# A two-layer MLP mixer kernel on one core: first loads ahead of the entry barrier on two rings, tile 0 started from its mean alone, two transposes fewer on TensorE, and a new order of the work

## The chip, the cores and the metric

The kernel runs on one core of one Trainium2 chip. The metric is the device time of one execution in microseconds; lower is better. The profiles record a span, from the first to the last instruction, which is 1.3 to 3.4 us shorter than the time of the same run. All runs use one core. A run is called fast or slow by its own time: slow if it is over 1.5% above the fastest run of the same kernel.

## The reference

```python
B, S, D, F = 1, 2048, 512, 1792            # bfloat16
h  = gelu(layernorm(x) @ w1)               # layer 1: D x D
c  = D // 4                                # four column groups of h are shifted along S
g0, g1, g2, g3 = shift(+1), shift(-1), shift(+2), shift(-2)
x1 = x + concat([g0, g1, g2, g3]) @ w2     # "mix"
out = x1 + gelu(layernorm(x1) @ w3) @ w4   # layer 2: "up" D x F, "down" F x D
```

S is worked on in 16 tiles of 128 rows. Layer 1 uses tile numbers 0 to 15, layer 2 the numbers 16 to 31 for the same rows (16 is row tile 0 of layer 2).

## The kernel before

The kernel lists operations, orders them on each engine with a small scheduling model, and emits them with semaphores. TensorE (PE) follows a hand-given script: `up1:N` and `up2:N` are the up-projections of the N-th group of tiles of layer 1 and layer 2 (the groups used below are single tiles at first, up to `up1:5` and `up2:1`), `mix:N` and `down:N` the products with w2 and w4 for row tile N. Each up-projection needs its normalised tile transposed, and there are two ways to do that. A tile named `ty:N` in the script is transposed on PE (four 128x128 matmuls against an identity, then a copy out of PSUM). Every other tile is transposed by a DMA that SyncE issues:

```python
if q not in pe_tp:                          # not named in the script
    pg.add("sp", f"tp{q}",
           lambda e: e.dma_start(xT[:, :, P * t : P * (t + 1)], xn_buf[:, slot(q), :], transpose=True),
           reads=[(("xn", slot(q)), q)], writes=[(("xT", t, c), layer) for c in range(DC)], queue="tp")
```

The order of the loads (all on SyncE) and the start of the script of PE:

```python
NAT = (1,)          # this tile is only centred; its scale is applied after its matmul ("by rows")
LOADS = """
x0 x2 x1 w1a w1b x3 x4-5 w2 w3 w4a tp17 w4b x6-7 x8-11 x12-15 tp8
"""
SCRIPT = """
warm:11 ty:1 ty:0 ty:2 up1:1 up1:0 th:1 up1:2 ty:3 mix:0 ty:4 mix:1 up1:3-4 mix:2 ty:16 mix:3 up2:0 up1:5
up2:1 mix:4 down:0-1 up2:2 up1:6-7 mix:6 down:3 down:2 mix:5 up1:8 ...          [cut]
"""
```

The tile in `NAT` is multiplied "by rows" (the row matmuls below), with its result not yet transposed; `th:N` transposes that result on PE. So before has six PE transposes of inputs (tiles 0 to 4 and 16); tile 5's up-projection stands behind the first of layer 2 (`up2:0`). `warm:11` are 11 matmuls on zeros. `emit` appends everything behind the entry barrier that the framework puts at the start of a program:

```python
for op in prog.seq:
    ...                                     # waits for what it needs
    ins = op.fn(engs[e])
    ins.then_inc(sems[op.stream], inc)
```

Of the kernel before, what the change touches and what calls it, by code (L numbers as in the profile page):

```python
# [6 lines left out]
P = 128  # L7
# [5 lines left out]
ENGINES = ["sp", "act", "pe", "dve", "pool"]  # L13

class Op:


    def __init__(self, name, eng, fn, reads, writes, dur, queue):
        self.name, self.eng, self.fn = name, eng, fn
        self.reads, self.writes = list(reads), list(writes)  # L20
        self.dur, self.queue = dur, queue
        self.idx = 0
        self.prio = 1e9
        self.first = None
        self.lag = 0.0

class Program:



    HOP = {"pe": 190.0, "dve": 160.0, "act": 230.0, "pool": 200.0, "sp": 70.0}
    LOOK = {"dve": 300.0, "act": 300.0}
    DUE = 6000.0

# [14 lines left out]
    def order(self):  # L49
# [13 lines left out]
        preds = [set() for _ in self.ops]  # L63
        for op in self.ops:
            d = preds[op.idx]
# [9 lines left out]
        order_only = set()  # L75
# [23 lines left out]
        while stack:  # L99
            i = stack.pop()  # L100
# [8 lines left out]
        if self.DUE:  # L109
# [15 lines left out]
            for i in reversed(topo):  # L125
# [7 lines left out]
                op.prio = late  # L133
        for op in self.ops:
            if op.first is not None:
                op.prio = op.first
# [4 lines left out]
        self.preds = preds  # L141
        npend = [len(d) for d in preds]
        ready = [0.0] * len(self.ops)
        cands = {e: [] for e in ENGINES}
        for op in self.ops:
            if npend[op.idx] == 0:
                cands[op.eng].append(op)
        free = {e: 560.0 for e in ENGINES}
        qfree = moved = 0.0
        turned = False  # L150
        out = []
        while len(out) < len(self.ops):
            best = None
            for e in ENGINES:
                if cands[e]:
                    t = max(free[e], min(ready[o.idx] for o in cands[e]))
                    if best is None or t < best[0]:
                        best = (t, e)
            t, e = best
            look = self.LOOK.get(e, 1.0)  # L160
            op = min((o for o in cands[e] if ready[o.idx] <= t + look), key=lambda o: (o.prio, o.idx))
            cands[e].remove(op)
            start = max(free[e], ready[op.idx])
            op.start = start
            if op.queue is None:
                done = free[e] = start + op.dur
            else:
                free[e] = start + (1300.0 if op.queue == "tp" else (1000.0 if e == "pool" else 460.0))
                if op.queue == "tp":
                    done = max(start + 2500.0, qfree + 1750.0)  # L170
                    qfree = max(qfree, start + 1400.0) + 600.0
                    turned = True
                else:
                    qfree = max(qfree, start + 1600.0) + op.dur
                    if turned and not op.name.startswith("out"):
                        qfree += 700.0
                        turned = False
                    moved += op.dur / 2900.0
                    done = qfree + op.lag + (350.0 if op.name.startswith("out") else min(1150.0, 250.0 + 900.0 * moved))
            out.append(op)  # L180
            for j in succs[op.idx]:
                npend[j] -= 1
                o = self.ops[j]
                hop = 70.0 if op.queue else (self.HOP[e] if o.eng != e else (0.0 if e == "pe" else 120.0))
                if (op.idx, j) not in order_only:
                    ready[j] = max(ready[j], done + hop)
                if npend[j] == 0:
                    cands[o.eng].append(o)
        self.seq = out
        for a, b in order_only:  # L190
            preds[b].discard(a)
        self.total = max(free.values())
        return out

GROUPS = {1: (1, 1, 1, 1, 1, 1, 2, 2, 2, 2, 2), 2: (1, 1, 2, 4, 4, 4)}
NORM = {5: "pool", 7: "act", 10: "pool", 11: "act", 18: "act", 19: "pool", 20: "pool"}
EVAC = {1: "both", 4: "both", 16: "dve"}
SQRT = ()
STAT_ACT = (1, 5, 6, 16, 18, 21)
HALF = ()  # L200
TAIL = (256, 128, 128)
VPE = {3: "pool", 4: "pool", 5: "pool", 6: "pool", 18: "pool", 19: "pool", 21: "pool"}
NMR = {1: "pool", 4: "pool", 5: "pool", 18: "pool", 20: "pool", 21: "pool"}
NAT = (1,)
HEV = {1: "dve", 4: "dve"}
LOADS = """
x0 x2 x1 w1a w1b x3 x4-5 w2 w3 w4a tp17 w4b x6-7 x8-11 x12-15 tp8
"""
SCRIPT = """
warm:11 ty:1 ty:0 ty:2 up1:1 up1:0 th:1 up1:2 ty:3 mix:0 ty:4 mix:1 up1:3-4 mix:2 ty:16 mix:3 up2:0 up1:5  # L210
up2:1 mix:4 down:0-1 up2:2 up1:6-7 mix:6 down:3 down:2 mix:5 up1:8 mix:8 mix:7 up1:9 mix:9-10 up1:10 mix:12
mix:11 up2:3 mix:14-15 up2:4 mix:13 down:5-6 down:9 down:7-8 down:4 up2:5 down:10 down:12 down:14 down:11
down:13 down:15
"""

def bass_standalone__mixer_s_mlp__prompt_kernel(nc, x, w1, w2, w3, w4, out):
# [14 lines left out]
    with ExitStack() as es:  # L231
# [62 lines left out]
        def load(item):  # L294
            name, _, eng = item.partition("@")
            eng = eng or "sp"
            if name[0] == "x":
# [8 lines left out]
                else:  # L306
                    yield pg.add(eng, f"dma_x{t0}",
                                 lambda e: e.dma_start(x_sb[:, t0:t1, :], xt[:, t0:t1, :]),
                                 writes=[(("x", t, hh), 0) for t in range(t0, t1) for hh in (0, 1)],
                                 dur=(t1 - t0) * 380.0, queue=eng)  # L310
            else:
# [6 lines left out]
                             writes=[((name[:2], c), 0) for c in range(c0, c1)],  # L318
                             dur=(c1 - c0) * P * src.shape[1] * 2 / 345.0, queue=eng)
                op.lag = 900.0 if name[:2] == "w2" else 0.0  # L320
                yield op
# [300 lines left out]
        pe_tp = {n for kind, n in steps if kind in ("tp", "ty")}  # L622
        queue = []
        for item in LOADS.split():
            if item[:2] == "tp":
                if int(item[2:]) not in pe_tp:
                    queue.append(item)
            else:
                for op in load(item):
                    op.first = len(queue) - 100  # L630
                    if op.eng == "sp":
                        queue.append(op.name)
        for t in range(NT):
            ln(1, t)
        for kind, n in steps:
# [10 lines left out]
            else:  # L646
                for _ in mm_up(int(kind[2]), n):
                    pass
        pg.line(queue)
        pg.order()  # L650
        emit(nc, es, pg)

def emit(nc, es, prog):
# [4 lines left out]
    for op in prog.seq:  # L658
        if op.queue is not None:
            op.stream = ("dma", ndma)  # L660
            sems[op.stream] = es.enter_context(nc.semaphore(f"sem_dma{ndma}"))
            ndma += 1
        else:
            op.stream = op.eng
    know = {e: {} for e in ENGINES}
    implied = {}
    count = {}
    last_write, readers = {}, {}
    for op in prog.seq:
# [19 lines left out]
        for s, v in sorted(needs.items(), key=lambda sv: -sv[1]):  # L689
# [6 lines left out]
            k[s] = max(k.get(s, 0), v)  # L696
        ins = op.fn(engs[e])
        inc = 1 if op.queue is None else 16
        ins.then_inc(sems[op.stream], inc)
# [6 lines left out]
        for res, ver in op.writes:  # L706
            last_write[res] = (op.stream, val, ver)
            readers[res] = []
    for op in prog.seq:
        if op.name.startswith("out_dma"):  # L710
            nc.sync.wait_ge(sems[op.stream], 16)
# [28 lines left out]
```

## Time and profile before

| | before |
|---|---|
| time, median of 4 runs | 137.95 us (136.35 to 138.11) |
| span of the profile | 135.2 us |
| PE busy | 97% |
| PE uninterrupted in the chain of waits | from 16.2 to 133.3 us |

The timeline of before for PE (start in us, duration in us, line, operation, count, and the idle time before with what ended it):

```profile
1.17 4.15 PE L604 MATMUL o_ps<-zeros 128*128 128x512 bf16 x11 [1.17 <-DVE zeros L281]
5.23 1.25 PE L437 MATMUL y_ps<-ident,xn_buf 128*128 128x128 bf16 x12
6.49 1.02 PE L455 MATMUL y_ps<-w_sb,xnT 128*128 128x512 bf16 x4
...
10.36 1.02 PE L551 MATMUL o_ps<-w_sb,hT 128*128 128x512 bf16 x4 [0.49 <-DVE vpe L349]
...
12.31 1.95 PE L511 MATMUL y_ps<-xnT,w_sb 128*128 128x128 bf16 x32
...
16.04 7.31 PE L511 MATMUL y_ps<-xnT,w_sb 128*128 128x128 bf16 x128
```

The warm-up ends near 5.3 us, the first real matmul starts at 6.49, the first mix at 10.36, and layer 2 at about 16. From there PE never stops. The chain of waits of before says the same (start, duration, what):

```profile
15.34 0.86 PE o_ps L551 x4
16.21 7.15 PE y_ps L511 x128
...
115.11 18.21 PE o_ps L580 x112
```

So only the head and the tail can be shortened. The first bn_stats on VectorE, and the issue table (size of one, median us from issue to landing):

```profile
2.83 1.29 DVE L363 BATCH_NORM_STATS2 st<-x_sb 128x6 f32<-128x512 bf16 x2 [1.71 <-DMA x_sb<-in_x_dram]
```

```profile
w_sb<-in_w_dram SPq DMA_DIRECT2D x1, 1792.0 KB, 10.3
...
xnT<-xn_buf SPq DMA_TRANSPOSE x26, 2.5
```

### The profile page before, as it was taken

What the parts mean: (1) busy time and instruction counts of PE and PEld (TensorE: products, weight loads), DVE (VectorE), ACT (ScalarE), POOL (GpSimd) and SP (SyncE); (2) the same over time, 40 slices, a digit from 0 to 9 for tenths busy, and PEclk for the clock granted to TensorE, in tenths of its full rate; (3) what the DMA queues carried; (4) which work ended last, traced back from release to release, by engine and by line L of the source; (5) the groups of instructions that cost most, each with busy time, mean ns of one, the idle gap of its engine ahead of it and who ended that gap; (6) DMA issues with size and microseconds to landing.
All of it is one profiled execution on the core that took longest, in us unless ns stands there. A gap on an engine that the chain in (4) does not pass through costs nothing.

```text
span 135.2 us, 2125 instructions
## 1 busy us (share of the span) xinstructions
PE 131.5 (97%) x855; PEld 73.5 (54%) x855; DVE 58.0 (43%) x164; ACT 49.4 (37%) x68; POOL 22.9 (17%) x52
## 2 busy tenths in 40 slices
PE   6999999999999999999999999999999999999994
PEld 2476799448874466644444444444444444444463
DVE  2986750799936359995008200622202200032222
ACT  4786377613941053325552555100000666300000
POOL 2355242233561011151000200100000000000000
DMA  4899979955654510404500120031110200011112
GB/s 120 283 314 379 298 114 330 298 87 116 122 112 83 116 41 0 82 0 84 110 0 0 39 43 0 0 78 39 39 39 13 67 2 0 0 39 39 39 39 78
DMA packets 22344, 12.44 MB, mean 92 GB/s; under 512 B 14912, under 2 KB 21824, under 8 KB 22336
## 3 DMA queue, kind: packets, MB, share of 16 engines
q1 hardware_dynamic: 21904, 12.19, 36.4%
q10 hardware_dynamic: 432, 0.13, 0.4%
q8 instruction: 6, 0.10, 0.3%
q14 instruction: 2, 0.02, 0.0%
HBM read 6.82 MB, written 2.10 MB: 66 GB/s over the span
## 4 chain that ended last, share of the span: by engine, by line
PE 95%; DVE 2%; POOL 1%; issue 1%; DVEq 0%
PE y_ps L511 44%; PE o_ps L580 36%; PE o_ps L551 10%; PE o_ps L604 3%; POOL rstd L381 1%; PE y_ps L437 1%; DVE st L363 0%; POOL vpe L370 0%; DVE xn_buf L393 0%; DVE mv L345 0%; DVE vpe L349 0%; DVE o_sb L588 0%; DVE zeros L281 0%; DVE xnT L443 0%; DVE mv L365 0%
## 5 line engine op out<-in xcount | busy, mean ns | idle before, releaser
L511 PE MATMUL y_ps<-xnT,w_sb 128*128 128x128 bf16 (+2 forms) x496 | 63.6, 288 | 0.0
L511 PEld LDWEIGHTS y_ps<-xnT,w_sb 128*128 128x128 bf16 x496 | 40.7, 98 | 23.0 <-issue 0.4
L580 PE MATMUL o_ps<-w_sb,h2T 128*128 128x512 bf16 (+2 forms) x252 | 49.1, 355 | 0.0
L526 ACT ACTIVATE h2T<-y_ps 128x1024 bf16<-128x1024 f32 (+2 forms) x29 | 28.8, 995 | 44.0 <-PE y_ps L511 44.0
L580 PEld LDWEIGHTS o_ps<-w_sb,h2T 128*128 128x128 bf16 x252 | 23.6, 98 | 25.2
L588 DVE TENSOR_TENSOR o_sb<-o_ps,x_sb 128x512 bf16<-128x512 f32 (+2 forms) x18 | 11.4, 632 | 39.6 <-PE o_ps L580 37.6
L381 POOL TENSOR_TENSOR rstd<-vpe,neghalf 128x1 f32<-128x1 f32 x32 | 17.5, 558 | 59.7 <-DVE vpe L370 41.9
L562 DVE TENSOR_TENSOR x_sb<-o_ps,x_sb 128x512 bf16<-128x512 f32 x13 | 8.9, 690 | 24.9 <-PE o_ps L551 24.9
L363 DVE BATCH_NORM_STATS2 st<-x_sb 128x6 f32<-128x512 bf16 x26 | 17.5, 686 | 1.9 <-DMA x_sb<-in_x_dram 1.7
L551 PE MATMUL o_ps<-w_sb,hT 128*128 128x512 bf16 x64 | 15.8, 379 | 0.5 <-DVE vpe L349 0.5
L393 DVE TENSOR_SCALAR xn_buf<-x_sb,mv,rstd 128x512 bf16<-128x512 bf16 x24 | 9.6, 410 | 3.4 <-POOL rstd L381 2.7
L526 ACT ACTIVATE hT<-y_ps 128x512 bf16<-128x512 f32 (+1 forms) x10 | 8.1, 809 | 7.9 <-PE y_ps L511 7.8
L551 PEld LDWEIGHTS o_ps<-w_sb,hT 128*128 128x128 bf16 x64 | 6.0, 98 | 6.1 <-DVE vpe L349 0.6
L338 ACT ACTIVATE junk<-x_sb 128x512 bf16<-128x512 bf16 x6 | 3.7, 624 | 9.5 <-DVE x_sb L558 9.4
L604 PE MATMUL o_ps<-zeros 128*128 128x512 bf16 x11 | 4.2, 552 | 1.2 <-DVE zeros L281 1.2
L365 DVE BATCH_NORM_AGGREGATE mv<-st 128x2 f32<-128x6 f32 x26 | 4.1, 173 | 0.3
L370 DVE TENSOR_SCALAR vpe<-mv 128x1 f32<-128x1 f32 x23 | 3.1, 149 | 0.3
L604 PEld LDWEIGHTS o_ps<-zeros 128*128 128x128 bf16 x11 | 1.4, 132 | 3.5 <-issue 2.2
L405 POOL TENSOR_SCALAR xn_buf<-x_sb,rstd,nmr 128x512 bf16<-128x512 bf16 x4 | 3.1, 768 | 0.3
L442 ACT ACTIVATE xnT<-y_ps 128x512 bf16<-128x512 bf16 (+1 forms) x5 | 2.4, 513 | 1.1 <-PE y_ps L437 1.1
L402 ACT ACTIVATE xn_buf<-x_sb,nmr,rstd 128x512 bf16<-128x512 bf16 x3 | 2.4, 806 | 1.1 <-DVE nmr L398 1.1
L558 DVE SCALAR_TENSOR_TENSOR x_sb<-o_ps,x_sb 128x512 bf16<-128x512 f32 x3 | 2.1, 690 | 1.3 <-PE o_ps L551 1.3
(33 smaller groups left out, 20.6 us busy)
## 6 DMA issues: line engine op xcount, KB each, us to landing
out_dram<-o_sb SPq DMA_DIRECT2D x15, 128.0 KB, 1.7
w_sb<-in_w_dram SPq DMA_DIRECT2D x1, 1792.0 KB, 10.3
w_sb<-in_w_dram SPq DMA_DIRECT2D x2, 896.0 KB, 9.5
x_sb<-in_x_dram SPq DMA_DIRECT2D x2, 512.0 KB, 8.1
x_sb<-in_x_dram SPq DMA_DIRECT2D x4, 128.0 KB, 2.1
w_sb<-in_w_dram SPq DMA_DIRECT2D x2, 256.0 KB, 3.1
x_sb<-in_x_dram SPq DMA_DIRECT2D x2, 256.0 KB, 4.7
w_sb<-in_w_dram SPq DMA_DIRECT2D x1, 512.0 KB, 6.2
```

Source lines behind the costliest of these rows:

```text
L338: (lambda d: (lambda e: e.activation(d, src, ACT_F.Square, accum_out=sums[:, q, 1:2])))(junk[:, b, :]),
L363: pg.add("dve", f"bnst{q}", lambda e: e.bn_stats(st6[:, q, :], src), reads=rs, writes=[(("st6", q), 0)], dur=605)
L365: pg.add("dve", f"bnag{q}", lambda e: e.bn_aggr(mv[:, q, :], st6[:, q, :]), reads=[(("st6", q), 0)], writes=[(("mv", q), 0)], dur=75)
L381: lambda e: e.tensor_tensor(col(rstd), col(vpe), neghalf[:], ALU.pow),
L393: lambda e: e.tensor_scalar(dst, src, mv[:, q, 0:1], rstd[:, q : q + 1], ALU.subtract, ALU.mult),
L511: ins = e.matmul(y_ps[:, p, W * i : W * (i + 1)], wsb[:, dc, P * fc : P * (fc + 1)], src[:, dc, P * t0 : P * t0 + W], start=(dc == 0), sto ...
L526: (lambda d, s: (lambda e: e.activation(d, s, ACT_F.Gelu_apprx_tanh)))(dst, ysrc),
L551: ins = e.matmul(dst, hT[:, j, c0 : c0 + P], w2_sb[:, j, :], start=(j == 0), stop=(j == DC - 1))
L562: f = lambda e: e.tensor_tensor(x1_sb[:, t, :], dst, x_sb[:, t, :], ALU.add)
L580: ins = e.matmul(dst, h2T[:, fc, P * t : P * (t + 1)], w4_sb[:, fc, cs], start=(fc == 0), stop=(fc == FC - 1))
L588: (lambda d, c: (lambda e: e.tensor_tensor(o_sb[:, oi, c], d, x1_sb[:, t, c], ALU.add)))(dst, cs),
L604: ins = e.matmul(o_ps[:, b, :], zeros[:, 0:P], zeros[:], start=True, stop=True)
```

## The change

Its intent: start the loads before the entry barrier and from two issuers (each issuing engine has a queue of its own, called its ring below; `@act` in the list of loads means ScalarE's), begin PE's real work with a tile that needs only its mean, save PE two transposes, and let a search find the rest of the order with a finer model of the DMA rings.

```diff
+    BEGIN = {"sp": 30.0, "act": 150.0, "pe": 400.0, "dve": 150.0, "pool": 450.0}
+    ENTRY = (1900.0, 2150.0)
 ...                                          [the scheduling model is rewritten; cut]
-GROUPS = {1: (1, 1, 1, 1, 1, 1, 2, 2, 2, 2, 2), 2: (1, 1, 2, 4, 4, 4)}
+GROUPS = {1: (1, 1, 1, 1, 1, 1, 2, 4, 1, 1, 2), 2: (1, 1, 2, 4, 4, 4)}
 ...                                          [NORM, EVAC, VPE, NMR, BIAS tables; cut]
-STAT_ACT = (1, 5, 6, 16, 18, 21)
-NAT = (1,)
+STAT_ACT = (0, 2, 6, 8, 10, 11, 12, 13, 23, 24, 25, 26, 28)
+NAT = (0,)
 LOADS = """
-x0 x2 x1 w1a w1b x3 x4-5 w2 w3 w4a tp17 w4b x6-7 x8-11 x12-15 tp8
+x1@act x0 x2@act w1b w1a x4 w2b@act w2a x3 x5 w3@act tp1 tp1 tp15 tp0 x8-10@act x14-15@act x13 x11-12@act
+tp1 x6-7@act w4@act
 """
 SCRIPT = """
-warm:11 ty:1 ty:0 ty:2 up1:1 up1:0 th:1 up1:2 ty:3 mix:0 ty:4 mix:1 up1:3-4 mix:2 ty:16 mix:3 up2:0 up1:5
+warm:3 warm:1 ty:0 up1:0 ty:1-2 th:0 up1:1-2 mix:0 ty:3 mix:1 up1:3-4 mix:2 up1:5 mix:3-4 up2:0-2 up1:6
 ...
+    listed = nc.m.functions[0].blocks[0].instructions
+    entry = next(i for i, ins in enumerate(listed) if type(ins).__name__ == "InstDrain")
 ...
+        if op.start < prog.ENTRY[0]:
+            ahead = len(listed)
 ...
+    listed[entry:ahead] = listed[body:ahead] + listed[entry:body]
```

The two PE transposes that go are those of tiles 4 and 16.

More of the change, by code (lines that the diff above doesn't have):

```diff
@@ L24, in __init__ @@
         self.first = None
-        self.lag = 0.0
 class Program:
-    HOP = {"pe": 190.0, "dve": 160.0, "act": 230.0, "pool": 200.0, "sp": 70.0}
+    HOP = {"pe": 200.0, "dve": 155.0, "act": 220.0, "pool": 120.0, "sp": 70.0}
     LOOK = {"dve": 300.0, "act": 300.0}
-    DUE = 6000.0
+    DUE = 3377.81
+    BEGIN = {"sp": 30.0, "act": 150.0, "pe": 400.0, "dve": 150.0, "pool": 450.0}
+    ENTRY = (1900.0, 2150.0)
     def __init__(self):
@@ L134, in order @@
         for op in self.ops:
+            op.prio += BIAS.get(op.name, 0.0)
             if op.first is not None:
@@ L141, in order, with place @@
         self.preds = preds
-        npend = [len(d) for d in preds]
+        out = self.place(succs, order_only)
+        for a, b in order_only:
+            preds[b].discard(a)
+        return out
+    def place(self, succs, order_only):
+        npend = [len(d) for d in self.preds]
         ready = [0.0] * len(self.ops)
@@ L147, in order, with finish @@
                 cands[op.eng].append(op)
-        free = {e: 560.0 for e in ENGINES}
-        qfree = moved = 0.0
-        turned = False
+        free = dict(self.BEGIN)
+        rings = {"sp": [], "act": []}
+        clock = moved = self.total = 0.0
         out = []
-        while len(out) < len(self.ops):
-            best = None
-            for e in ENGINES:
-                if cands[e]:
-                    t = max(free[e], min(ready[o.idx] for o in cands[e]))
-                    if best is None or t < best[0]:
-                        best = (t, e)
+        def finish(limit):
+            nonlocal clock
+            while True:
+                heads = {e: r[0] for e, r in rings.items() if r}
+                if not heads:
+                    return None
+                live = [e for e in heads if heads[e][0] <= clock]
+                later = min([h[0] for h in heads.values() if h[0] > clock], default=1e18)
+                if not live:
+                    if later > limit:
+                        return None
+                    clock = later
+                    continue
+                first = min(live, key=lambda e: heads[e][1])
+                step = heads[first][1] * len(live)
+                ends = clock + step <= min(later, limit)
+                if not ends:
+                    step = min(later, limit) - clock
+                for e in live:
+                    heads[e][1] -= step / len(live)
+                clock += step
+                if ends:
+                    return rings[first].pop(0)[2]
+                if clock >= limit:
+                    return None
@@ new lines, in release, with land @@
+        def release(op, o, at):
+            npend[o.idx] -= 1
+            if at is not None:
+                ready[o.idx] = max(ready[o.idx], at)
+            if npend[o.idx] == 0:
+                cands[o.eng].append(o)
+        def land(op):
+            nonlocal moved
+            if op.queue == "tp":
+                at = max(clock + 500.0, op.start + 2450.0)
+            elif op.name.startswith("out"):
+                at = clock + 300.0
+                self.total = max(self.total, at)
+            else:
+                moved += op.dur
+                at = clock + 650.0 + min(450.0, 0.25 * moved) + (1200.0 if op.dur > 1400.0 else 0.0)
+            for j in succs[op.idx]:
+                if (op.idx, j) not in order_only:
+                    release(op, self.ops[j], at + 30.0)
@@ L159, in order @@
+        while len(out) < len(self.ops):
+            while True:
+                best = None
+                for e in ENGINES:
+                    if cands[e]:
+                        t = max(free[e], min(ready[o.idx] for o in cands[e]))
+                        if best is None or t < best[0]:
+                            best = (t, e)
+                op = finish(best[0] if best else 1e17)
+                if op is None:
+                    break
+                land(op)
             t, e = best
@@ L163, in order @@
             start = max(free[e], ready[op.idx])
+            if start >= self.ENTRY[0]:
+                start = max(start, self.ENTRY[1])
             op.start = start
-            if op.queue is None:
-                done = free[e] = start + op.dur
-            else:
-                free[e] = start + (1300.0 if op.queue == "tp" else (1000.0 if e == "pool" else 460.0))
-                if op.queue == "tp":
-                    done = max(start + 2500.0, qfree + 1750.0)
-                    qfree = max(qfree, start + 1400.0) + 600.0
-                    turned = True
-                else:
-                    qfree = max(qfree, start + 1600.0) + op.dur
-                    if turned and not op.name.startswith("out"):
-                        qfree += 700.0
-                        turned = False
-                    moved += op.dur / 2900.0
-                    done = qfree + op.lag + (350.0 if op.name.startswith("out") else min(1150.0, 250.0 + 900.0 * moved))
@@ L180, in order @@
-            out.append(op)
-            for j in succs[op.idx]:
-                npend[j] -= 1
-                o = self.ops[j]
-                hop = 70.0 if op.queue else (self.HOP[e] if o.eng != e else (0.0 if e == "pe" else 120.0))
-                if (op.idx, j) not in order_only:
-                    ready[j] = max(ready[j], done + hop)
-                if npend[j] == 0:
-                    cands[o.eng].append(o)
+            out.append(op)
+            if op.queue:
+                tp = op.queue == "tp"
+                free[e] = start + (1300.0 if tp else 460.0)
+                rings[e].append([start + (1400.0 if tp else 1000.0), 600.0 if tp else op.dur, op])
+                for j in succs[op.idx]:
+                    if (op.idx, j) in order_only:
+                        release(op, self.ops[j], None)
+            else:
+                free[e] = start + op.dur
+                for j in succs[op.idx]:
+                    o = self.ops[j]
+                    hop = self.HOP[e] if o.eng != e else (0.0 if e == "pe" else 120.0)
+                    release(op, o, None if (op.idx, j) in order_only else start + op.dur + hop)
@@ L189, in order @@
+        while (op := finish(1e17)) is not None:
+            land(op)
         self.seq = out
-        for a, b in order_only:
-            preds[b].discard(a)
-        self.total = max(free.values())
-        return out
-GROUPS = {1: (1, 1, 1, 1, 1, 1, 2, 2, 2, 2, 2), 2: (1, 1, 2, 4, 4, 4)}
-NORM = {5: "pool", 7: "act", 10: "pool", 11: "act", 18: "act", 19: "pool", 20: "pool"}
-EVAC = {1: "both", 4: "both", 16: "dve"}
+        return out
+GROUPS = {1: (1, 1, 1, 1, 1, 1, 2, 4, 1, 1, 2), 2: (1, 1, 2, 4, 4, 4)}
@@ L198 @@
+NORM = {6: "pool", 7: "act", 8: "pool", 10: "pool", 12: "act", 13: "pool", 14: "pool", 20: "pool", 21: "pool", 23: "pool", 24: "pool", 25: "pool", 27: "act", 28: "act", 29: "act", 31: "pool"}
+EVAC = {0: "dve", 1: "both", 4: "dve", 5: "dve", 6: "dve", 8: "dve", 9: "both", 10: "dve", 12: "both", 13: "both", 15: "both", 19: "dve", 20: "dve", 22: "dve", 23: "dve", 24: "dve", 26: "dve", 27: "both", 28: "dve", 29: "dve", 30: "dve", 31: "dve"}
 SQRT = ()
-STAT_ACT = (1, 5, 6, 16, 18, 21)
+STAT_ACT = (0, 2, 6, 8, 10, 11, 12, 13, 23, 24, 25, 26, 28)
@@ L200 @@
 HALF = ()
 TAIL = (256, 128, 128)
-VPE = {3: "pool", 4: "pool", 5: "pool", 6: "pool", 18: "pool", 19: "pool", 21: "pool"}
-NMR = {1: "pool", 4: "pool", 5: "pool", 18: "pool", 20: "pool", 21: "pool"}
-NAT = (1,)
-HEV = {1: "dve", 4: "dve"}
+VPE = {1: "pool", 2: "pool", 3: "pool", 4: "pool", 6: "pool", 7: "pool", 9: "pool", 10: "pool", 12: "pool", 13: "pool", 14: "pool", 17: "pool", 18: "pool", 19: "pool", 21: "pool", 22: "pool", 25: "pool", 26: "pool", 27: "pool", 28: "pool", 30: "pool"}
+NMR = {1: "pool", 2: "pool", 5: "pool", 8: "pool", 10: "pool", 11: "pool", 13: "pool", 15: "pool", 18: "pool", 21: "pool", 22: "pool", 25: "pool", 26: "pool", 29: "pool", 31: "pool"}
@@ L206 @@
+NAT = (0,)
+HEV = {1: "dve", 2: "dve", 3: "dve"}
+BIAS = {"bnst19": 1806.98, "bnst3": 919, "bnst5": -1528.57, "bnst6": -755, "mean16": -61, "msq15": -99, "nmr2": -416.496, "rstd11": -131, "rstd18": 1533, "rstd22": 450, "ssq4": 250, "vpe0": -916.1, "vpe11": 651, "vpe19": 1017.92, "vpe7": 264, "x1_0": 1177}
 LOADS = """
-x0 x2 x1 w1a w1b x3 x4-5 w2 w3 w4a tp17 w4b x6-7 x8-11 x12-15 tp8
+x1@act x0 x2@act w1b w1a x4 w2b@act w2a x3 x5 w3@act tp1 tp1 tp15 tp0 x8-10@act x14-15@act x13 x11-12@act
+tp1 x6-7@act w4@act
@@ L208 @@
 """
 SCRIPT = """
-warm:11 ty:1 ty:0 ty:2 up1:1 up1:0 th:1 up1:2 ty:3 mix:0 ty:4 mix:1 up1:3-4 mix:2 ty:16 mix:3 up2:0 up1:5
-up2:1 mix:4 down:0-1 up2:2 up1:6-7 mix:6 down:3 down:2 mix:5 up1:8 mix:8 mix:7 up1:9 mix:9-10 up1:10 mix:12
-mix:11 up2:3 mix:14-15 up2:4 mix:13 down:5-6 down:9 down:7-8 down:4 up2:5 down:10 down:12 down:14 down:11
-down:13 down:15
+warm:3 warm:1 ty:0 up1:0 ty:1-2 th:0 up1:1-2 mix:0 ty:3 mix:1 up1:3-4 mix:2 up1:5 mix:3-4 up2:0-2 up1:6
+down:1 mix:5 up1:7 mix:6 down:3 mix:9 up1:8 mix:7-8 up1:9 mix:11 mix:10 up1:10 mix:12 down:0 up2:3 mix:15
@@ L214 @@
+mix:14 up2:4 mix:13 down:5 down:4 down:2 down:9 up2:5 down:8 down:7 down:13 down:6 down:11 down:10 down:12
+down:14-15
 """
@@ L309, in load @@
                                  writes=[(("x", t, hh), 0) for t in range(t0, t1) for hh in (0, 1)],
-                                 dur=(t1 - t0) * 380.0, queue=eng)
+                                 dur=(t1 - t0) * 430.0, queue=eng)
             else:
@@ L318, in load @@
                              writes=[((name[:2], c), 0) for c in range(c0, c1)],
-                             dur=(c1 - c0) * P * src.shape[1] * 2 / 345.0, queue=eng)
-                op.lag = 900.0 if name[:2] == "w2" else 0.0
+                             dur=(c1 - c0) * P * src.shape[1] * 2 / (300.0 if src.shape[1] == D else 380.0), queue=eng)
                 yield op
@@ L622, in bass_standalone__mixer_s_mlp__prompt_kernel @@
         pe_tp = {n for kind, n in steps if kind in ("tp", "ty")}
-        queue = []
-        for item in LOADS.split():
+        queues = {"sp": [], "act": []}
+        for i, item in enumerate(LOADS.split()):
             if item[:2] == "tp":
                 if int(item[2:]) not in pe_tp:
-                    queue.append(item)
+                    queues["sp"].append(item)
             else:
                 for op in load(item):
-                    op.first = len(queue) - 100
-                    if op.eng == "sp":
-                        queue.append(op.name)
+                    op.first = i - 100
+                    queues[op.eng].append(op.name)
         for t in range(NT):
@@ L648, in bass_standalone__mixer_s_mlp__prompt_kernel @@
                     pass
-        pg.line(queue)
+        for queue in queues.values():
+            pg.line(queue)
         pg.order()
@@ L664, in emit @@
             op.stream = op.eng
+    listed = nc.m.functions[0].blocks[0].instructions
+    entry = next(i for i, ins in enumerate(listed) if type(ins).__name__ == "InstDrain")
+    body = len(listed)
+    ahead = body
     know = {e: {} for e in ENGINES}
```

## The prediction

> **What bounds the kernel.** TensorE (PE). The page gives PE 97% of a 135.2 us span; the chain of waits puts 95% of the span on PE. In that chain PE is never held up after 16.2 us: 117.1 us of matmuls run to 133.3 us, at 0.86 us for four 512-column matmuls and 12.1 us for 56 up-projection matmuls of 512 columns. From these durations I count about 124.9 us of useful matmuls, 7.9 us of them before 16.2 us. So what can be won lies in the first 16.2 us (8.3 us there are warm-up, transposes and waits) and in the 1.9 us tail, which the change leaves alone.
>
> **The head, by the timeline.** Nothing is issued before about 0.72 us (the entry barrier). SyncE issues the first three x loads from 0.73 us at 0.45 us each; the first bn_stats starts at 2.83 us, the ScalarE sum of tile 1 at 3.88 us. The 11 warm-up matmuls fill 1.17 to 5.3 us, spaced 0.43 us until about 4.5 us. The first real matmul starts at 6.49 us. The chain up to 10.36 us runs through normalisation on VectorE and GpSimd, not loads.
>
> **What the change does.**
> 1. First loads issued before the barrier: about 0.7 us earlier; with two issuers x0, x1, x2 leave by about 0.6 us instead of 2.1. The Trainium skill ("DMA: Bandwidth & Descriptors", Issuing engines are not separate DMA queues) says a second issuer saves only issue time, as all share the same 16 DMA engines; at the roughly 300 GB/s of the early slices I expect w1 landed near 5 us, against 5 to 5.6.
> 2. Tile 0 comes first, needing only its mean (ScalarE 0.63 + 0.19 us, VectorE 0.15 and 0.35): first transpose near 4.1 to 4.6 us, first real matmul near 5.2 us, instead of 6.49. -1.3 us.
> 3. Two PE transposes fewer (one left to the DMA): 2 x 0.22 = -0.4 us, part of it hidden in waits.
> 4. Costs: tile 3 and w2 land later (ScalarE issues loads between early activations), tiles 4 and 5 depend on DMA transposes (2.5 us each in the issue table).
> 5. Warm-up falls from 11 to 4 matmuls: about 1.7 us, then about 2 us idle. The skill ("TensorE: Matmul & The Clock Gate", part 1) says the clock is half-rate until a sustained window of about 3.4 us; this trace agrees: spacing 0.43 us for 3.3 us, then shorter. So the first real work may run at half rate, up to about 1.5 us lost, partly inside other waits.
>
> Sum: about -2 us ideal; +0.5 us for late landings and the cold clock on average. Nothing changes after 20 us.
>
> **Predicted time: 136.0 us** (before 137.82), range 134.0 to 137.8. Faster by over 2%: 0.25; within 2%: 0.67; slower: 0.08.
>
> **What would show it.** First DMA issue near 0 us in the timeline; first real matmul at 5.0 to 5.5 us; chain of waits: PE without interruption from about 16 to 17 us with one more up-projection tile and one more mix done by then; four PE transposes. A cold clock would show as 1.7 us for tile 0's four row matmuls instead of 0.86.
>
> **What would make it wrong.** ScalarE delayed by DMA issues or its 1.28 us table load, so tile 0's sum starts after 4 us; PE cold until about 10 us; waits for DMA transposes before the second-layer groups at 16 to 30 us; or the head filling completely (over 3 us gained).

## More of the kernel before

The view of one source line gives the spread that the issue table hides. For the 26 DMA transposes of before:

```profile
L411 SPq DMA_TRANSPOSE xnT<-xn_buf x26: 1189/1264/2149, 12.2 to 87.9; - x26
DMA to landing us min/median/max: 2.4/2.5/7.6
```

The first of them (issued at 12.2 us, while w3 and w4 are still being loaded) took 6.8 us and landed at 18.9. That is late, but in this order nobody is waiting for it: it is tile 5's, whose up-projection stands behind `up2:0`. Of the 26, four were issued before 27 us and took 3.2 to 7.6 us; the other 22 took 2.4 to 4.0.

Table by stage of before (us, the stretch's length, then busy us of each engine with instruction counts, granted PE clock, share of DMA time, GB/s):

```profile
10.00:15.00 5.00, 4.64 (x49) 3.25 (x50) 3.37 (x13) 3.29 (x8) 2.39 (x5) 1.00 1.01 378
15.00:20.00 5.00, 5.00 (x80) 4.53 (x79) 3.19 (x11) 2.38 (x4) 1.63 (x5) 1.00 1.06 156
20.00:25.00 5.00, 5.00 (x70) 4.05 (x67) 0.89 (x3) 3.92 (x7) 0.95 (x2) 1.00 1.05 328
```

## The result and the profile after

The time went up, to 144.11 us (median of 4 runs, 143.44 to 144.49), against 137.95 of before. The ratio is 1.048, with a 95% interval of 1.041 to 1.055. A ratio is the mean time of one kernel's fast runs over that of the other's of the same rounds, so it is not quite the ratio of the medians. The result lies outside the predicted range.

The timeline of after for PE:

```profile
0.53 1.89 PE L658 MATMUL o_ps<-zeros 128*128 128x512 bf16 x4 [0.53 <-DVE zeros L336]
4.16 0.61 PE L491 MATMUL y_ps<-ident,xn_buf 128*128 128x128 bf16 x4 [1.74 <-DVE xn_buf L443]
5.38 1.86 PE L509 MATMUL y_ps<-w_sb,xnT 128*128 128x512 bf16 x4 [0.61 <-DVE mv L396]
...
10.97 0.81 PE L605 MATMUL o_ps<-w_sb,hT 128*128 128x512 bf16 x3
...
12.70 1.06 PE L565 MATMUL y_ps<-xnT,w_sb 128*128 128x128 bf16 x16
17.41 1.89 PE L565 MATMUL y_ps<-xnT,w_sb 128*128 128x128 bf16 x16 [3.65 <-DMA xnT<-xn_buf]
...
28.78 11.16 PE L565 MATMUL y_ps<-xnT,w_sb 128*128 128x128 bf16 x128 [0.51 <-DMA xnT<-xn_buf]
```

The first real matmul is at 5.38 us, as predicted. But tile 0's four row matmuls take 1.86 us, against 1.02 for those of tile 1 in before, and the first mix starts near 10.8, no earlier than in before (the line shows three of its four matmuls; the first is missing from the trace). Then, after tile 3, PE stands idle for 3.65 us for a DMA transpose, and the next matmuls also take twice as long (1.89 against 1.06 for the same 16). PE is uninterrupted only from 28.8 us. The chain of waits of after shows what it hangs on:

```profile
9.66 7.70 DMA xnT<-xn_buf
17.36 0.05 issue
17.41 1.89 PE y_ps L565 x16
19.29 1.72 PE o_ps L605 x4
...
23.25 5.48 DMA xnT<-xn_buf
28.73 0.05 issue
28.78 11.16 PE y_ps L565 x128
```

Tile 4's transpose is issued at 9.66 and lands at 17.36. The issue table still gives 2.5 us as the median; the view of the source line, for the three transposes issued between 9 and 15.5 us (tiles 4, 5 and 16), gives 7.7 to 10.1:

```profile
xnT<-xn_buf SPq DMA_TRANSPOSE x28, 2.5
```

```profile
L465 SPq DMA_TRANSPOSE xnT<-xn_buf x3: 1233/1258/1274, 9.7 to 14.7; - x3
...
  PE y_ps L565: 4.0, 2
...
DMA to landing us min/median/max: 7.7/8.7/10.1
```

By stage, after (columns as above; the clock is the third number from the end). The clock of the cold start does not show in this column: it is 1.00 in the stages before 10 us too, where the row matmuls took 1.86 us.

```profile
10.00:15.00 5.00, 3.65 (x43) 2.52 (x41) 3.84 (x9) 2.39 (x4) 1.43 (x3) 1.00 1.05 288
15.00:20.00 5.00, 2.59 (x19) 2.04 (x20) 0.32 (x1) 0.60 (x1) 0.00 (x0) 0.62 1.14 263
20.00:25.00 5.00, 4.45 (x27) 2.77 (x27) 3.15 (x7) 2.26 (x7) 1.58 (x4) 0.70 1.20 206
```

From 15 to 20 us VectorE, ScalarE and GpSimd are almost idle as well. The kernel gives each of them its instructions in a fixed order, and the next ones belong to tiles behind the stall. That is how one late transpose makes the next ones late: tile 17's transpose leaves only at 23.25, after the delayed mix 2 in VectorE's order. PE's clock falls to 0.62 after the idle stretch. The Trainium skill ("TensorE: Matmul & The Clock Gate", part 1) describes this: half rate after an idle window of about 3.4 us, full rate after a busy one. The trace agrees with the two states, not with the length: the matmuls ran at half rate until about 22.9 us, 5.5 us after the work resumed, and the granted clock was 0.50 already from 16.2 us, 2.4 us into the idle stretch.

The start holds another surprise. The first instruction on ScalarE that reads x in after:

```profile
2.80 0.63 ACT L387 ACTIVATE junk<-x_sb 128x512 bf16<-128x512 bf16 x1 [0.29 <-PEq L786]
```

It was released by the barrier (the releaser "PEq" is PE's sequencer), although the trace shows x0 landed at 2.17 us. In before the barrier opens at 0.72 us and x0 lands at 2.81. The loads now go ahead of the barrier, but so do four warm-up matmuls (until 2.42 us) and ScalarE's 1.28 us table load (its first activation ends at 2.51), and the barrier opens only when they are done. The statistics therefore start at 2.80 instead of 2.83.

### The profile page after: what moved, and what is told of

Its sections match the earlier page's. It is cut to its first block, busy times and chain, and to the rows that moved or that the text cites. A ratio compares the mean times of both kernels' runs of the same rounds, so it can differ in the third digit from the quotient of the medians.

```text
span 143.0 us, 2121 instructions
## 1 busy us (share of the span) xinstructions
PE 132.9 (93%) x828; PEld 73.8 (52%) x840; DVE 53.2 (37%) x150; ACT 57.6 (40%) x94; POOL 31.5 (22%) x73
## 4 chain that ended last, share of the span: by engine, by line
PE 83%; DMA 9%; DVE 3%; issue 1%; POOL 1%; ACT 1%
PE y_ps L565 39%; PE o_ps L634 34%; DMA xnT<-xn_buf 9%; PE o_ps L605 8%; PE y_ps L509 1%; DVE st L417 1%; PE y_ps L491 1%; ACT junk L387 1%; DVE xnT L497 1%; DVE x_sb L616 0%; POOL rstd L435 0%; POOL vpe L424 0%; DVE xn_buf L447 0%; DVE xn_buf L443 0%; DVE o_sb L642 0%
## 5 line engine op out<-in xcount | busy, mean ns | idle before, releaser
L565 PE MATMUL y_ps<-xnT,w_sb 128*128 128x128 bf16 (+2 forms) x493 | 65.9, 295 | 4.6 <-DMA xnT<-xn_buf 4.5
L605 PE MATMUL o_ps<-w_sb,hT 128*128 128x512 bf16 x60 | 16.2, 397 | 0.4 <-DVE mv L419 0.2
L580 ACT ACTIVATE hT<-y_ps 128x512 bf16<-128x512 f32 (+1 forms) x11 | 8.3, 752 | 18.5 <-PE y_ps L565 18.5
L417 DVE BATCH_NORM_STATS2 st<-x_sb 128x6 f32<-128x512 bf16 x19 | 12.9, 686 | 2.5 <-PEq L786 2.3
L447 DVE TENSOR_SCALAR xn_buf<-x_sb,mv,rstd 128x512 bf16<-128x512 bf16 x15 | 7.9, 524 | 5.2 <-POOL rstd L435 4.9
L459 POOL TENSOR_SCALAR xn_buf<-x_sb,rstd,nmr 128x512 bf16<-128x512 bf16 x11 | 8.5, 775 | 1.8 <-DVE nmr L452 1.7
L392 ACT ACTIVATE junk<-x_sb 128x512 bf16<-128x512 bf16 x13 | 8.1, 621 | 1.6 <-DVE x_sb L612 1.6
L424 POOL TENSOR_SCALAR vpe<-mv 128x1 f32<-128x1 f32 x13 | 3.1, 236 | 17.9 <-DVE mv L419 14.5
L456 ACT ACTIVATE xn_buf<-x_sb,nmr,rstd 128x512 bf16<-128x512 bf16 x5 | 4.0, 809 | 5.3 <-POOL nmr L452 2.8
L387 ACT ACTIVATE junk<-x_sb 128x512 bf16<-128x512 bf16 x8 | 5.0, 623 | 0.3 <-PEq L786 0.3
L612 DVE SCALAR_TENSOR_TENSOR x_sb<-o_ps,x_sb 128x512 bf16<-128x512 f32 x5 | 3.5, 692 | 1.4 <-PE o_ps L605 1.4
L491 PE MATMUL y_ps<-ident,xn_buf 128*128 128x128 bf16 x16 | 2.0, 287 | 1.7 <-DVE xn_buf L443 1.7
L491 PEld LDWEIGHTS y_ps<-ident,xn_buf 128*128 128x128 bf16 x16 | 1.6, 130 | 3.4 <-DVE xn_buf L443 2.6
```

Of the source, the lines that this page charges most:

```text
L387: (lambda d: (lambda e: e.activation(d, src, ACT_F.Copy, accum_out=sums[:, q, 0:1])))(junk[:, b, :]),
L392: (lambda d: (lambda e: e.activation(d, src, ACT_F.Square, accum_out=sums[:, q, 1:2])))(junk[:, b, :]),
L417: pg.add("dve", f"bnst{q}", lambda e: e.bn_stats(st6[:, q, :], src), reads=rs, writes=[(("st6", q), 0)], dur=605)
L447: lambda e: e.tensor_scalar(dst, src, mv[:, q, 0:1], rstd[:, q : q + 1], ALU.subtract, ALU.mult),
L459: f = lambda e: e.tensor_scalar(dst, src, rstd[:, q : q + 1], nmr[:, q : q + 1], ALU.mult, ALU.add)
L565: ins = e.matmul(y_ps[:, p, W * i : W * (i + 1)], wsb[:, dc, P * fc : P * (fc + 1)], src[:, dc, P * t0 : P * t0 + W], start=(dc == 0), sto ...
```

## The experiments

Theories. **T1**: a DMA transpose issued while bulk loads are in flight lands 6 to 10 us later, not 2.5; the change made PE depend on such transposes. **T2**: the second ring is to blame (transposes on the SyncE ring beside loads on the ScalarE ring). **T3**: the transposes are late for another reason. Besides these, the half clock could be a cause of its own: after the stall, or at the start, where only 4 warm-up matmuls are left. The diffs below show the changed part of a line only.

### e1: tiles 4 and 5 back on PE

```diff
-ty:3 mix:1 up1:3-4 mix:2 up1:5
+ty:3 mix:1 ty:4 up1:3-4 ty:5 mix:2 up1:5
```

> The kernel after, with tiles 4 and 5 of the first layer transposed on PE instead of by DMA. Theory T1 (DMA transposes issued while bulk loads are in flight land 7 to 10 us later instead of 2.5, and PE starves for tiles 4 and 5): the 3.65 us idle before the up-projection of tile 4 and the half clock after it go away, second layer starts near 19 to 20 us instead of 25, time 137 to 140 us. Rival T2 (PE starves because of something else in the new order, tile 4 only shows it): another wait takes its place in the same 13 to 20 us, time still above 142.

Measured: 143.91 us, ratio 1.046 (1.036 to 1.056). The wait for tile 4 is gone, and another has taken its place. The timeline of e1 for PE:

```profile
23.80 15.90 PE L565 MATMUL y_ps<-xnT,w_sb 128*128 128x128 bf16 x184 [4.40 <-DMA xnT<-xn_buf]
```

This is layer 2's first tile (16), whose transpose was issued at 15.58 and landed at 23.67, 8.1 us later. By the words put down beforehand it is the rival that came true (called T2 there, but not the T2 above): another wait took the place, and the time stayed above 142. The time prediction of T1 failed; its mechanism is still there, one transpose further on. Tile 16 is the other PE transpose that the change removed.

### e2: dummy matmuls in the stall

Seventeen matmuls on zeros are put between the up-projections of tiles 3 and 4, outside the schedule, so that the order of all other engines is unchanged.

```diff
+        if op.name == "up1_3_0":
+            s, v, _ = last_write[("x1", 0)]
+            engs["pe"].wait_ge(sems[s], v)
+            for _ in range(17):
+                prog.fill(engs["pe"])       # one 128x512 matmul on zeros
```

> The kernel after, with 17 dummy matmuls on zeros put into the idle time of PE before tile 4's up-projection; order of all other engines unchanged. If the half clock after the stall costs time of its own (T1): the matmuls at 17 to 23 us run at full rate, the row of them takes about 2.6 us less, tile 17's normalisation comes earlier, and the time falls by 1 to 2.5 us to about 142 us. If the half clock is only a symptom and the transposes set the pace: within 0.5 us of 144.1.

Measured: 144.74 us, ratio 1.051 (1.039 to 1.062). PE's mean granted clock was 1.000 in all four runs (0.976 to 0.988 in those of after), and no time was gained. The profile is of a slow run, and tile 4's transpose landed even later in it (20.14 us). The three fast runs (143.48, 144.68, 144.80; mean 144.32 against 144.04 of after) show no gain either. So the half clock after the stall is a symptom: the transposes set the pace.

### e3: w3 behind the transposes

w3 and all later loads go on the SyncE ring: w3 behind tiles 4 and 5, the rest behind tiles 16 and 17.

```diff
-w2a x3 x5 w3@act tp1 tp1 tp15 tp0 x8-10@act x14-15@act x13 x11-12@act
-tp1 x6-7@act w4@act
+w2a x3 x5 tp4 tp5 w3 tp16 tp17 x6-7 w4 x8-10 x11-12 x13 x14-15
```

> The kernel after, with w3 and all later loads on the SyncE ring behind the DMA transposes of tiles 4 and 5 (w3) and of tiles 16 and 17 (the rest). T1: with no bulk load in flight the transposes of tiles 4 and 5 land within 2.5 to 4 us of their issue, PE is not idle over 1 us before tile 4; w3 then lands later, near 18 to 19 us, and the time is 137 to 140 us. If the transposes are slow for another reason than bulk loads (T3): they still take over 6 us to land and the idle stays.

Measured: 148.25 us, ratio 1.080 (1.070 to 1.089), so the time was mispredicted by 8 us. The transposes behaved as T1 says. The view of the source line in e3 for the two issued between 9 and 12.1 us:

```profile
L464 SPq DMA_TRANSPOSE xnT<-xn_buf x2: 1220/1245/1270, 9.5 to 10.9; - x2
...
DMA to landing us min/median/max: 2.4/2.5/2.5
```

The same two tiles, issued at about the same time as in after (9.54 and 10.90 us, against 9.66 and 11.36), land in 2.5 us when nothing else is in flight; T3 falls. The time was lost elsewhere: w3 came at 20.97, and tiles 18 and 19, issued from 25.65 behind w4, again took 7.8 and 6.2 us, which ends in a wait of 6 us in the timeline of e3 for PE:

```profile
34.05 10.12 PE L564 MATMUL y_ps<-xnT,w_sb 128*128 128x256 bf16 x72 [6.02 <-ACT junk L391]
```

The releaser named there is a ScalarE instruction long done; the transposes landed at 33.42 and 33.92. So the new order of the loads had only moved them into the way of later transposes.

### e4: the same fault put into before

```diff
-ty:3 mix:0 ty:4 mix:1
+ty:3 mix:0 mix:1
```

> The kernel before, with only tile 4's PE transpose left to the DMA, all on the one SyncE ring. T1 (any bulk load in flight, whatever ring): tile 4's transpose lands 6 to 8 us after its issue, near 18 us, PE idles 3 to 5 us before tile 4 and then runs at half clock for some us; time 142 to 146 us. Rival T2 (only the interleaving of two rings makes the transposes slow): it lands in 2.5 to 3.5 us and the time stays within 1 us of 137.9.

Measured: 145.60 us median, with one fast run at 142.88 (before in the same rounds: 137.97 median) and three slow ones at 145.47 to 146.08. The fast run alone is 3.6% above before's median; it is one run, so it has no interval. Its mean granted clock was 0.988 (0.998 to 1.000 in the fast runs of before), which fits a stall with half clock after it there too. The profile (of a slow run) shows the wait on the single ring, in the source view for two transposes and in the timeline for PE:

```profile
  PE y_ps L511: 5.6, 1
...
DMA to landing us min/median/max: 6.0/6.9/7.9
```

```profile
18.71 1.89 PE L511 MATMUL y_ps<-xnT,w_sb 128*128 128x128 bf16 x16 [5.64 <-DMA xnT<-xn_buf]
```

One `ty:4` less in before reproduces the stall and the doubled matmul time without a second ring, so T2 is not needed. The packet records of the trace show one difference, though: on the one ring the transpose's first packet comes at 14.70 us, when the ring has nearly worked off the loads ahead of it; on two rings, in after, transpose and loads run side by side (see the last section).

### e5: only the barrier part, in before

The three first x loads, constants and 3 of the 11 warm-up matmuls go ahead of the barrier.

```diff
-warm:11 ty:1
+warm:3 warm:8 ty:1
+        if op.start < 1900.0:
+            ahead = len(listed)
+    listed[entry:ahead] = listed[body:ahead] + listed[entry:body]
```

> The kernel before with one thing of the change alone: the three first x loads, the constants and 3 of the 11 warm-up matmuls put ahead of the entry barrier; order on every engine unchanged. If the earlier start of the loads carries through to the chain of the head: first bn_stats about 0.7 us earlier in the span than 2.83, time 0.4 to 0.9 us less than before. If the head is bound by later loads or by the engines: same within 0.3 us.

Measured: 137.14 us, ratio 0.998 (0.993 to 1.003): the same. bn_stats starts at 2.31 instead of 2.83 (at the barrier's release), but the halves of w1, issued after a barrier that now opens near 2.3, land at 5.06 and 5.76, as in before (5.03 and 5.83). In the profile layer 2 starts at 15.62 instead of 16.04, a gain too small for these runs to show.

### e6: all transposes of the loading time on PE

```diff
-ty:3 mix:1 up1:3-4 mix:2 up1:5 mix:3-4 up2:0-2
+ty:3 mix:1 ty:4 up1:3-4 ty:5 mix:2 ty:16 up1:5 mix:3-4 ty:17 up2:0-2
```

> The kernel after with the transposes of tiles 4 and 5 of layer 1 and of tiles 0 and 1 of layer 2 (16, 17) all on PE, so that no DMA transpose is needed until about 25 us. T1: the 4 us wait of e1_ty45 for tile 16 goes too, no DMA-transpose wait over 1 us is left before 26 us, second layer starts near 19.5 us, time 139 to 140.5 us; what is left above before is the half clock of the first 9 to 10 us. If another wait takes its place: above 142 us.

Measured: 139.55 us, ratio 1.015 (1.008 to 1.022). The first DMA transpose is issued at 20.25. The timeline of e6 for PE:

```profile
19.07 6.42 PE L565 MATMUL y_ps<-xnT,w_sb 128*128 128x128 bf16 x112
25.92 8.02 PE L565 MATMUL y_ps<-xnT,w_sb 128*128 128x256 bf16 x72 [0.43 <-ACT junk L387]
```

Layer 2 starts at 19.07 instead of 24.98 and only 0.43 us of waiting is left there. The mean of the fast runs falls from 144.04 (after) to 139.52: 4.5 of the roughly 6.4 us (144.04 less 137.65, the mean of before's fast runs beside e6; after was run in other rounds).

### e7: e6 with a longer warm-up

```diff
+        if op.name == "tp0":
+            for _ in range(5):
+                prog.fill(engs["pe"])
```

> e6_ty4_5_16_17 with 5 more warm-up matmuls between the barrier and the first transpose; order of every other engine unchanged. If the short warm-up costs time (half clock until 9 to 10 us): the four row matmuls of tile 0 take about 0.9 us instead of 1.86, second layer starts 1.5 to 2.5 us earlier than in e6, time 137 to 138.5 us. If the half clock is hidden in waits for data: within 0.5 us of e6.

Measured: 138.41 us, ratio 1.006 (1.000 to 1.013); 1.07 us less than e6 by the means of the fast runs (138.45 and 139.52). The timeline of e7 for PE:

```profile
6.15 1.18 PE L509 MATMUL y_ps<-w_sb,xnT 128*128 128x512 bf16 x4 [0.61 <-DVE mv L396]
```

The row matmuls take 1.18 instead of 1.89 us, but start 0.2 us later than in e6, where they waited for w1, and 0.8 us later than in after: the cold filler is itself in the way. Layer 2 starts at 18.56 us, 0.5 us earlier than in e6 and not the expected 1.5 to 2.5. With no more DMA stalls the short warm-up seems to cost about 1 us, but the fast runs of e6 (138.96 to 140.01) and e7 (137.74 to 139.22) overlap, so this is not settled.

### e8: exactly the two removed transposes back

```diff
-ty:3 mix:1 up1:3-4 mix:2 up1:5
+ty:3 mix:1 ty:4 up1:3-4 mix:2 ty:16 up1:5
```

> The kernel after with exactly the two PE transposes back that the change takes away (tiles 4 and 16). If those two alone are the cause: second layer starts near 19.5 us, time 139 to 140.5. If the new order (tile 5's up-projection ahead of the second layer, its transpose by DMA under load) shares in it: PE waits 2 to 5 us for tile 5's transpose, landing at 17 to 20 us, time 140.5 to 143.

Measured: 140.11 us in one fast run, 144.41 to 145.92 in three slow ones (median 144.88). The profile is of a slow run: the timeline for PE shows tile 5 stuck, its transpose issued at 11.85 and landed at 22.01.

```profile
22.06 1.89 PE L565 MATMUL y_ps<-xnT,w_sb 128*128 128x128 bf16 x16 [5.95 <-DMA xnT<-xn_buf]
```

This is inconclusive as to shares. The fast run agrees with the first expectation (139 to 140.5), while the slow profile shows the stall of the second. The mean granted clock tells the same: 1.000 in the fast run, 0.976 to 0.988 in the three others, so here "slow" most likely means that the transpose came late, as it did in three of four runs. What it does show is that in this order tile 5 can become the next victim.

### e9, e11 and e12: attempts at a version better than both

e9 takes the change's start (barrier, two rings for the first loads, tile 0 first), 3 extra warm-up matmuls behind the barrier and, from the first mixes on, the order of before, with most of its tables and its order of the later loads; e11 puts w3 and the first half of w4 on the ScalarE ring; e12 is e11 with 5 instead of 3 extra warm-up matmuls.

```diff
 e9:  x1@act x0 x2@act w1b w1a x4 w2b@act w2a x3 x5 w3 w4a tp17 w4b x6-7 x8-11 x12-15
 e11: x1@act x0 x2@act w1b w1a x4 w2b@act w2a x3 x5 w3@act w4a@act tp17 w4b x6-7 x8-11 x12-15
+SCRIPT: warm:3 warm:1 ty:0 up1:0 ty:1-2 th:0 up1:1-2 mix:0 ty:3 mix:1 ty:4 up1:3-4 mix:2 ty:16 mix:3 up2:0 up1:5 ...
```

> A version meant to beat both: the change's start (first loads ahead of the barrier on two rings, tile 0 first by its mean, 3 more warm-up matmuls after the barrier) with everything after the first two mixes as in before: PE transposes of tiles 4 and 16, tile 5 behind the second layer's first tile, loads of w3 and w4 on the SyncE ring as in before. Head: first real matmul near 5.4 us, second layer's first tile 0.3 to 1.0 us earlier than before's 16.2, no wait for a DMA transpose over 0.5 us; time 0.3 to 1.0 us less than before. If the earlier start is taken back by later landings of w2 and of tiles 3 to 5: same as before within 0.3 us.

> e9_hybrid with w3 and the first half of w4 on the ScalarE ring instead of the SyncE ring, nothing else moved on VectorE, GpSimd and PE. If sharing the DMA engines with another ring is what stretches a DMA transpose (packets taken in turn): the first two transposes, issued near 11 to 15 us, land at another time than in e9 by over 1.5 us and the bulk loads beside them slow down too. If only the bytes ahead of them count, whatever ring: they land within 1 us of e9's and the time is within 0.5 us of e9's.

> e11_hybrid_two_rings with 5 instead of 3 extra warm-up matmuls; order of all other engines unchanged. If the half clock of the head takes the gain of the earlier start: tile 0's row matmuls take 1.0 to 1.3 us instead of 1.86, the first mix starts near 10.4 us instead of 10.88, time 0.3 to 0.8 us less than e11, about 138.2, so not below before, because the filler itself delays the first transpose by about 0.7 us. If the clock does not matter there: same as e11 within 0.2 us.

Measured:

| | median us | ratio to before | 95% interval |
|---|---|---|---|
| e9 | 141.91 (two fast runs: 139.27, 140.96) | 1.018 | 1.011 to 1.025 |
| e11 | 138.77 | 1.007 | 1.002 to 1.011 |
| e12 | 138.77 | 1.010 | 1.004 to 1.015 |

None beats before. In the profile of e9 (a slow run) the first mix waits for the second half of w2, as the timeline for PE shows. The profile names no releaser, but the trace has this load landing at 12.51:

```profile
12.82 0.81 PE L604 MATMUL o_ps<-w_sb,hT 128*128 128x512 bf16 x3 [2.48 <-issue]
```

That 256 KB load took 8.7 us in e9, where w3 was issued 0.15 us before it on the other ring, and 3.7 us in e11, where w3 stands behind it on its own ring. The first DMA transpose, on the other hand, landed at 17.16 in e9 and at 17.43 in e11, each just after the first half of w4 (16.66 and 16.88), with bulk on its own ring in one and on the other ring in the other. For the transposes the ring made no difference of note, as the second expectation says, but the pair tests little: both were issued late (13.21 and 13.48 us), most of e11's packets ran when the loads' packets were through (half of them by 15.09), and the e9 profile is of a slow run. The times do differ, by 1.4 us between the means of the fast runs (140.12 and 138.74), where that expectation had 0.5.

e12 does not beat e11 (means of the fast runs 138.59 and 138.74, from different rounds): its row matmuls take 1.44 instead of 1.86 us, but they start at 6.14 instead of 5.38, and the first mix at 11.01 instead of 10.88. The expected 0.3 to 0.8 us did not come. A shorter half-clock stretch is paid for with the filler's own time. In both, layer 2 starts about half a us later than the 16.04 of before: at 16.70 in e12, and in the timeline of e11 for PE at

```profile
16.57 7.31 PE L564 MATMUL y_ps<-xnT,w_sb 128*128 128x128 bf16 x128
```

### e10: after with only the longer warm-up

> The kernel after with 5 more warm-up matmuls between the barrier and the first transpose and nothing else. If the waits for DMA transposes set the pace in after (T1), warming PE gains nothing there: time within 0.7 us of 144.1, although tile 0's row matmuls run at about 0.9 to 1.2 us instead of 1.86. If the cold start is a cause of its own in after: 1 to 2 us less.

Edit as in e7, on after. Measured: 145.18 us median, ratio 1.047 (1.041 to 1.053), as after. The mean of the two fast runs (143.56, 144.55) is 144.06, that of after 144.04. In after itself the cold start costs nothing that these runs show: the stalls absorb it. The timeline of e10 for PE:

```profile
15.87 1.07 PE L565 MATMUL y_ps<-xnT,w_sb 128*128 128x128 bf16 x16 [2.19 <-DMA xnT<-xn_buf]
...
20.14 1.35 PE L565 MATMUL y_ps<-xnT,w_sb 128*128 128x128 bf16 x16 [2.34 <-DMA xnT<-xn_buf]
```

Here tile 4 waits less (2.19 us), and tile 5 takes over (2.34 us). The clock fell again, to 0.66 in the stage from 20 to 25 us (third number from the end):

```profile
20.00:25.00 5.00, 4.64 (x33) 2.87 (x35) 1.72 (x5) 2.43 (x7) 0.48 (x2) 0.66 1.14 300
```

### e13: before with five loads ahead of the barrier

As e5, with both halves of w1 too and 4 + 7 warm-up matmuls; order unchanged on every engine.

> The kernel before with its first five loads (x0, x2, x1, both halves of w1) ahead of the barrier, 4 of the 11 warm-up matmuls too; nothing reordered. If the earlier loads carry through: both halves of w1 and x3 land 0.4 to 0.7 us earlier than in before, PE is continuous from 15.5 to 15.8 us instead of 16.2, time 0.4 to 0.8 us less (ratio 0.994 to 0.997). If the head is bound by something else: ratio 0.998 to 1.002.

Measured: 137.33 us, ratio 0.996 (0.990 to 1.002). The halves of w1 land at 4.36 and 5.04 instead of 5.03 and 5.83, though x3 lands later (6.94 against 6.41), and layer 2 starts at 15.39 instead of 16.04 in the profile. The gain, some 0.5 us, has the expected size, but five rounds do not separate it from zero.

## Why the prediction was wrong, point by point

- **What bounds the kernel** was right: PE, with only the head to win. In after, too, PE runs on without a long wait once layer 2 has started (from 28.8 us).
- **Step 1**, loads 0.7 us earlier: right for the issue (0.00 us) and for the landings (x0 2.17, w1 5.18), wrong in what follows. The barrier moved from 0.72 to about 2.79 us, and the statistics start at 2.80 instead of 2.83. I had not counted the table load and warm-up among the work ahead of the barrier; with 3 warm-up matmuls there instead of 4, and the table load over by 1.4 us, it opened near 2.3 us (e5).
- **Step 2**, first transpose at 4.1 to 4.6, first real matmul near 5.2: measured 4.16 and 5.38. The gain was spent before the first mix (about 10.8 us against 10.36 in before).
- **Step 3**, two PE transposes fewer for -0.4 us: wrong in sign. Before does tiles 4 and 16 on PE while the loads run and puts tile 5 behind layer 2's first tile; e4 shows what tile 4 alone is worth: its one fast run is 4.9 us above the median of before.
- **Step 4 is the one that failed.** It said that "tiles 4 and 5 depend on DMA transposes (2.5 us each in the issue table)" and put "+0.5 us for late landings and the cold clock". The durations under load were 7.7, 8.7 and 10.1 us for tiles 4, 5 and 16; the prediction had not named tile 16 at all. PE was therefore uninterrupted only from 28.8 us, where the prediction had 16 to 17. The experiments show it from four sides: the same transposes land in 2.5 us with no bulk load in flight (e3), the same fault stalls before on one ring (e4), removing tiles 4 and 5 alone moves the stall to tile 16 (e1), and taking all four off the DMA recovers 4.5 us (e6). The median of 2.5 was of 26 transposes, 22 of them issued after 27 us, when the loads had landed or nearly so; the same source line's maximum in before was 7.6. The prediction did name "waits for DMA transposes before the second-layer groups at 16 to 30 us" as a way to be wrong, but gave slower by over 2% only 0.08.
- **Step 5**, cold clock, up to 1.5 us: a cost of perhaps 1.1 us where no stall hides it (e6 to e7, not settled), none to be seen in after itself (e10). The fear that the row matmuls would run at half clock was right.
- **Sum.** Of the roughly 6.4 us above before, 4.5 are the DMA-transpose waits and perhaps 1.1 the warm-up. What is left in e7, ratio 1.006 with an interval that reaches from 1.000 to 1.013, is not resolved.
- **Open.** Why a version of the start without both faults (e11, e12) is still not faster than before is only partly told: its row matmuls still run below the full clock, and its layer 2 starts at 16.6 to 16.7 us, not 16.04. The shares of tiles 4 and 16 against tile 5's new place could not be separated (e8).

## What to carry to other kernels

A duration taken from the median of a table holds for the conditions in which most of its calls ran. Before a change moves work into another stage, look up the spread and the calls that ran in that stage. A redundant-looking operation in a tuned kernel (two transposes on the busiest engine) may be what keeps that engine from waiting on something slower. Putting work ahead of a barrier also moves the barrier: count the slowest engine's work in front of it, not only the load that is meant to start early.

## What the Trainium skill lacked or had wrong

- "DMA: Bandwidth & Descriptors", DMA Transpose (X-bar), gives constraints but no duration, and no page gives one beside bulk loads (where a transpose is timed or rated, it is alone). Measured here for 128x512 bf16 (128 KB): 2.4 to 2.5 us from issue to landing with nothing else in flight, 7.7 to 10.1 us (after) and 6.0 to 7.9 us (e4) beside bulk loads.
- The same page, Queues, rings and completion order, says that a DMA engine takes turns between rings packet by packet. The packet records of after fit this once a transpose runs: from 12.5 to 18.5 us, 1022 transpose packets of 256 B ran beside 1045 packets of 1024 B or more of the other ring, about one for one. What the page does not tell is the late start: tile 4's transpose was issued at 9.66 and has no packet before 12.57, 2.9 us later, against 1.25 us with nothing else in flight (e3, issued at 9.54, first packet at 10.79). No run here tells why.
- The same page, Issuing engines are not separate DMA queues, says a second issuer saves only issue time. The choice of ring and order went with a different landing, too: 256 KB of w2 took 8.7 us in e9 and 3.7 us in e11 (the e9 profile is of a slow run, and w3's place in the issue order changed with its ring).
- "TensorE: Matmul & The Clock Gate", part 1, puts the half rate down to an idle window of about 3.4 us. Here the clock fell sooner: 2.4 us into the idle stretch in after, and to 0.66 in the stage from 20 to 25 us of e10, where no idle stretch was longer than 2.34 us.
- No page says that work moved ahead of the entry barrier delays it: it opened at 0.72 us in before, near 2.3 in e5 and at about 2.79 us in after.
